# Keys in three chunks of 128 and one of 64 instead of four of 112, with the 64s of two pairs of heads multiplied with their values together on quarters of the array

## The chip, the cores and the metric

One core of one Trainium2 chip runs the kernel. The metric is the device time of one execution in microseconds (us). TensorE (PE) multiplies matrices and has a row of its own for loading weights (PEld); VectorE (DVE), ScalarE (ACT) and GpSimd (POOL) work element by element; SyncE (SP) issues the DMAs of this kernel. Each engine takes its instructions in the order in which the program writes them and waits on semaphores for the others.

## The reference, cut to what matters

```
def _attn_ref(q, k, v):  # 4 batches, 12 heads, 448 positions, 64 wide
    scores = scale * np.matmul(q, k.transpose(0, 1, 3, 2)) - np.log(S)
    attn = 1.0 / (1.0 + np.exp(-scores))
    return np.matmul(attn, v)

x = attn_out, heads side by side: (4, 448, 768)
u = x + token mixing of rank 32 (U, V)        # _moe_ref
x = u + max(u @ w_ch1, 0) @ w_ch2             # 768 -> 3072 -> 768
...                                           # _moe2_ref: theta, cos and sin, two token matrices, w_ch
```

All of it is float32. The change is in the attention and in the small matmuls that the kernel weaves into it. The expression `attn @ v` sums over the 448 keys; in what order the keys stand in the chunks does not matter to that sum, as long as k and v are cut alike.

## The kernel before

The 48 heads are taken as 24 pairs p; a pair's two heads lie on partitions 0 to 63 and 64 to 127. The 448 keys of a pair are four chunks of CP = 112. In the loop over p, TensorE does for each pair:

- `TQ(p + 1)` and `TK(p + 2)`: four transposes each, which turn q and k so that the 64 channels lie on partitions. They write PSUM tiles of the tags `qx` (one bank) and `kk` (two banks), one buffer each; ACT and DVE then split the result into a high and a low part (`kh`, `kl`, `qh`, `ql`).
- `QK(p, half)`: scores of two chunks. Per chunk three products (high by high, high by low, low by high), each as two matmuls, one for each head, on the upper and the lower 64 rows of the array at once. ACT's sigmoid then writes the tile `A` of the chunk. The score tiles (`sc`, two banks) have two buffers.
- `AV(p - 1, c)`: for chunk c two float32 matmuls, one for each head, on the left and the right 64 columns of the array at once. They add up in one PSUM bank (`av`, one buffer) over the four chunks; after the last DVE copies the bank into `X`.
- `XN(p - 2)`: four transposes of `X` into a tile of the tag `qx`, copied by DVE to `xn`.
- In three of the iterations `U1` (24 small matmul rows into the tag `kk`, split by ACT and then by six DVE rows `pc` in `u1_lo`), and in nine (p = 9 to 11, 15 to 17, 21 to 23) `U2`: two matmuls into the two banks of a `kk` tile, which one DVE addition takes into `X`.
- two `early_step()`s: a step each of converting the weights of the next stage (rows L146 to L167 of ACT and DVE, L112 and L115 of POOL).

The order in an iteration is QK half 0, TQ, AV chunks 0 and 1, TK, a step, QK half 1, XN, U1 or U2, AV chunks 2 and 3, `u1_lo`, the loads of pair p + 3, a step. After the loop `split_u(0)` splits batch 0 of X (six rows of ACT, six of DVE), the last pair's four `AV` follow, then `split_u(1)`, `XN(22)`, the first product with w_ch1 (`ch1(0, 0)`), `XN(23)`, and so on. What comes after is the same program in both kernels.

`load_pair(p)` issues on SP, at one place in its order, two DMAs for k, two to four for q and one for v. The pairs 0, 1 and 2, then the U and V matrices, are loaded before the loop; pair 3 is loaded at the end of iteration 0, pair 4 at the end of iteration 1.

The changed lines, as before:

Of the kernel before, what the change touches and what calls it, by code (L numbers as in the profile page):

```python
# [24 lines left out]
def tile_kernel(  # L25
# [15 lines left out]
    nc = tc.nc  # L41
# [66 lines left out]
    def hi_act(o, i):  # L108
        nc.scalar.activation(o, i, AF.Copy)  # L109
# [10 lines left out]
    def lo_dve(o, i, h):  # L120
        nc.vector.tensor_sub(o, i, f(h))  # L121
# [190 lines left out]
    u_in = ap.tile([CP, 2, NC, R], F32, name="u_in")  # L312
    vcat = ap.tile([P, 2, S], F32R, name="vcat")

    q_t, k_t, v_t, qq_t, kk_t, A_t, av_t, xn_t = {}, {}, {}, {}, {}, {}, {}, {}

    def load_pair(p):
        b, hp = divmod(p, NH)
        h0 = 2 * hp
        qt = ap2.tile([CP, NC, 2, D], F32, tag="q", name=f"q_{p}", bufs=3)  # L320
        vt = ap1.tile([CP, 2, NC, D], F32, tag="v", name=f"v_{p}", bufs=4)
        kt = ap2.tile([CP, NC, 2, D], F32, tag="k", name=f"k_{p}", bufs=3)
        for h in range(2):
# [12 lines left out]
        nc.sync.dma_start(
            out=vt.rearrange("p h c d -> p h (c d)"),
            in_=v[b, h0:h0 + 2].rearrange("h (p c) d -> p h (c d)", p=CP),
        )
        q_t[p], k_t[p], v_t[p] = qt, kt, vt  # L340

    def TQ(p):
        ps = ps_a.tile([P, 512], F32, tag="qx", name=f"tq_{p}")
# [10 lines left out]
        qq_t[p] = (h_, l_)  # L354

    def TK(p):
        ps = ps_a.tile([P, 2, 512], F32, tag="kk", name=f"tk_{p}")
        t = k_t.pop(p)
        for c in range(NC):
            nc.tensor.transpose(  # L360
                ps[:, 0, c * CP:(c + 1) * CP], t[:, c].rearrange("p h d -> p (h d)"), ident[:CP, :CP]
            )
        h_ = ap2.tile([P, S], F32R, tag="kh", name=f"kh_{p}", bufs=3)
        l_ = ap2.tile([P, S], F32R, tag="kl", name=f"kl_{p}", bufs=3)
        kk_t[p] = (h_, l_)
        hi_act(h_, ps[:, 0, :S])
        lo_dve(l_, ps[:, 0, :S], h_)

    def QK(p, half):


        (kh, kl), (qh, ql) = kk_t[p], qq_t[p]
        for c in (2 * half, 2 * half + 1):
            ps = ps_b.tile([P, 2, 512], F32, tag="sc", name=f"sc_{p}_{c}", bufs=2)
# [6 lines left out]
            a = ap1.tile([CP, 2, S], F32, tag="A", name=f"A_{p}_{c}", bufs=6)  # L381
            nc.scalar.activation(a, ps[:CP, :, :S], AF.Sigmoid, bias=bias_s[:CP], scale=SCALE)  # L382
            A_t[p, c] = a

    def AV(p, c):
        b, hp = divmod(p, NH)
        if c == 0:
            if p < NP - 1:
                av_t[p] = ps_a.tile([P, 512], F32, tag="av", name=f"av_{p}")
            else:  # L390
                av_t[p] = ps_a.tile([P, 2, 512], F32, tag="kk", name=f"av_{p}")[:, 0]
        ps = av_t[p]
        for h in range(2):
            nc.tensor.matmul(  # L394
                ps[h * D:(h + 1) * D, :S], v_t[p][:, h, c, :], A_t[p, c][:, h, :],
                start=c == 0, stop=c == NC - 1,
            )
        if c == NC - 1:
            nc.vector.tensor_copy(X[:, hp, b * S:(b + 1) * S], ps[:, :S])
# [12 lines left out]
    pc_t, u1_t = {}, []  # L412

    def U1(b, p):
        ps = ps_a.tile([P, 2, 512], F32, tag="kk", name=f"p1_{b}")
        for c in range(NC):
            for g in range(3):
                nc.tensor.matmul(
                    ps[g * R:(g + 1) * R, 1, :2 * P], u_in[:, b % 2, c, :], xn_t[b][:, c, 2 * g * P:2 * (g + 1) * P],
                    start=c == 0, stop=c == NC - 1,  # L420
                )
        o = p.tile([P, DM], F32R, tag="pc", name=f"pc_{b}")
        for g in range(3):
            x = ps[g * R:(g + 1) * R, 1, :2 * P]
            sl = slice(2 * g * P, 2 * (g + 1) * P)
            for m in range(2):
                hi_act(o[m * R:(m + 1) * R, sl], x)
        pc_t[b] = o
        u1_t.append((ps, o))

    def u1_lo():

        while u1_t:
            ps, o = u1_t.pop()
            for g in range(3):
                x = ps[g * R:(g + 1) * R, 1, :2 * P]
# [104 lines left out]
    for p in range(NP):  # L541
        nx = p + 1 < NP
        QK(p, 0)
        if nx:
            TQ(p + 1)
        if p:
            AV(p - 1, 0)
            AV(p - 1, 1)
        if p + 2 < NP:
            TK(p + 2)  # L550
        if p:
            early_step()
# [7 lines left out]
        if b >= 0 and r < NK // 2:  # L560
# [362 lines left out]
```

## Time and profile before

| | us |
|---|---|
| median of 3 runs | 1248.75 (1247.99 to 1248.86) |
| the profiled execution | 1244.25 |
| span of its instructions | 1241.9 |
| attention loop, about | 9 to 202 of the span |
| PE busy | 1213.5 (98%) |

The rows further down come from the profiled execution; times in them are us from the start of its span. In a timeline row stand the start, the length, the engine, the line, the operation, out<-in, the shapes, how many instructions were merged, and in brackets the idle time before it with what ended it. A float32 matmul of `AV` leaves two rows for each instruction, so that one chunk of a pair is four rows. Matmul lengths hold a pipeline's depth, so the distance from start to start is the time that a matmul takes from its engine.

### The profile page before, as it was taken

The numbers are of one execution on the slowest core, as the hardware profiler recorded it, in microseconds if no ns is written. First come the engines' busy times: TensorE is split into PE (matmuls) and PEld (weight loads), VectorE is DVE, ScalarE is ACT, GpSimd is POOL, SyncE is SP. The second block draws the span as 40 slices with busy tenths as digits, with TensorE's granted clock in tenths as the row PEclk, the third lists the DMA queues.
The fourth block names the chain that finished last, engine by engine and source line by source line (L and its number), as shares of the span: only waits on it lengthen the run. The fifth ranks groups of instructions, "written<-read, shape, count | busy, mean of one in ns | idle before, by whom it ended". The sixth has DMA issues, their size and how long they took to land.

```text
span 1241.9 us, 15876 instructions
## 1 busy us (share of the span) xinstructions
PE 1213.5 (98%) x6546; PEld 1051.4 (85%) x6546; DVE 757.5 (61%) x863; ACT 376.4 (30%) x479; POOL 326.7 (26%) x182
## 2 busy tenths in 40 slices
PE   7999999999998989999999999999999999999998
PEld 4555556898888979999999999999999999999998
DVE  3466666458787786777778796967434642731222
ACT  5666665312121221212212121212113531620121
POOL 0112122315243342223324253433200521320000
PEclk9999999999999999999999999999999999999999
DMA  6454541002414141323232323423131000030111
GB/s 162 108 148 105 130 101 51 1 27 77 127 60 144 51 142 41 121 64 98 66 96 77 117 88 116 127 96 89 55 145 51 1 1 1 22 132 1 64 51 64
DMA packets 87783, 99.88 MB, mean 80 GB/s; under 512 B 48416, under 2 KB 77984, under 8 KB 87584
## 3 DMA queue, kind: packets, MB, share of 16 engines
q1 hardware_dynamic: 87712, 98.88, 26.0%
q8 instruction: 51, 0.84, 0.3%
q14 instruction: 20, 0.16, 0.0%
HBM read 80.71 MB, written 18.15 MB: 80 GB/s over the span
## 4 chain that ended last, share of the span: by engine, by line
PE 80%; DVE 10%; issue 8%; DMA 1%; ACT 1%; POOL 1%; SPq 0%; POOLq 0%; ACTq 0%; DVEq 0%
PE g L599 7%; PE g L598 7%; PE g L600 7%; PE y L620 7%; PE y L622 7%; PE y L621 7%; PE av L394 6%; PE sc L378 5%; PE y L810 3%; PE y L811 3%; PE y L809 3%; PE wc L732 2%; PE wc L736 2%; PE wc L733 2%; DVE X L624 2%
## 5 line engine op out<-in xcount | busy, mean ns | idle before, releaser
L620 PE MATMUL y<-gh,w 128*128 128x448 f32 x576 | 213.6, 371 | 16.6 <-DVE X L624 15.1
L622 PE MATMUL y<-gh,w 128*128 128x448 f32 x576 | 212.3, 369 | 0.0
L621 PE MATMUL y<-gl,w 128*128 128x448 f32 x576 | 212.2, 368 | 0.0
L598 PE MATMUL g<-uh,w 128*128 128x448 f32 x576 | 211.3, 367 | 0.0
L599 PE MATMUL g<-ul,w 128*128 128x448 f32 x576 | 211.0, 366 | 0.0
L600 PE MATMUL g<-uh,w 128*128 128x448 f32 x576 | 210.8, 366 | 0.0
L624 DVE TENSOR_TENSOR X<-y,X 128x896 f32<-128x896 f32 x144 | 156.3, 1087 | 87.4 <-PE y L622 86.0
L112 POOL TENSOR_TENSOR ca_w<-ca_w,w 128x768 f32<-128x768 f32 x48 | 94.6, 1970 | 387.4 <-ACT w L109 376.6
L605 ACT ACTIVATE gh<-g 128x896 fp32r<-128x896 f32 x48 | 44.1, 919 | 344.2 <-PE g L600 344.2
L620 PEld LDWEIGHTS y<-gh,w 128*128 128x128 f32 x576 | 109.0, 189 | 28.4 <-DVE X L624 17.9
L622 PEld LDWEIGHTS y<-gh,w 128*128 128x128 f32 x576 | 109.3, 190 | 9.1
L621 PEld LDWEIGHTS y<-gl,w 128*128 128x128 f32 x576 | 109.2, 190 | 8.8
L598 PEld LDWEIGHTS g<-uh,w 128*128 128x128 f32 x576 | 108.6, 189 | 9.4 <-issue 0.4
L599 PEld LDWEIGHTS g<-ul,w 128*128 128x128 f32 x576 | 108.5, 188 | 9.3 <-DVE ul L121 0.4
L600 PEld LDWEIGHTS g<-uh,w 128*128 128x128 f32 x576 | 108.4, 188 | 8.9
L606 DVE SCALAR_TENSOR_TENSOR gl<-g,gh 128x896 fp32r<-128x896 f32 x48 | 52.3, 1089 | 99.2 <-ACT gh L605 99.2
L382 ACT ACTIVATE A<-sc,bias_s 112x896 f32<-112x896 f32 x96 | 91.5, 1003 | 38.6 <-PE sc L378 38.4
L115 POOL TENSOR_TENSOR w<-ca_w,ws_w 128x768 fp32r<-128x768 f32 x48 | 93.4, 1947 | 3.8
L112 POOL TENSOR_TENSOR zl<-t,zh 128x768 fp32r<-128x768 f32 x23 | 42.7, 1878 | 161.3 <-ACT zh L109 161.3
L394 PE MATMUL av<-A,v 112*64 112x448 f32 x384 | 82.3, 551 | 0.0
L121 DVE TENSOR_TENSOR xl<-X,xh 128x768 fp32r<-128x768 f32 x28 | 31.7, 1136 | 67.8 <-ACT xh L109 67.8
L109 ACT ACTIVATE xh<-X 128x768 fp32r<-128x768 f32 x28 | 23.5, 842 | 155.9 <-PE wc L733 92.7
(148 smaller groups left out, 1982.8 us busy)
## 6 DMA issues: line engine op xcount, KB each, us to landing
ws_w<-in_moe_w_ch_dram SPq DMA_DIRECT2D x48, 768.0 KB, 4.6
k<-in_k_dram SPq DMA_DIRECT2D x48, 112.0 KB, 3.4
v<-in_v_dram SPq DMA_DIRECT2D x24, 224.0 KB, 2.9
ws_th<-in_moe_w_theta_dram SPq DMA_DIRECT2D x6, 768.0 KB, 4.4
th_d<-sp_th SPq DMA_DIRECT2D x6, 768.0 KB, 6.9
ws_wc<-in_moe_w_ch_dram SPq DMA_DIRECT2D x6, 768.0 KB, 5.1
wc_d<-sp_wc SPq DMA_DIRECT2D x6, 768.0 KB, 6.9
th_r<-th_d SPq DMA_DIRECT2D x6, 768.0 KB, 4.4
```

Of the source, the lines that this page charges most:

```text
L112: nc.gpsimd.tensor_sub(o, a, b)
L115: nc.gpsimd.tensor_add(o, a, b)
L378: nc.tensor.matmul(ps[:CP, h, :S], a[sl, c * CP:(c + 1) * CP], b[sl], start=n == 0, stop=n == 2)
L382: nc.scalar.activation(a, ps[:CP, :, :S], AF.Sigmoid, bias=bias_s[:CP], scale=SCALE)
L394: nc.tensor.matmul(ps[h * D:(h + 1) * D, :S], v_t[p][:, h, c, :], A_t[p, c][:, h, :], start=c == 0, stop=c == NC - 1,)
L598: nc.tensor.matmul(o, wh[:, sl], uh_t[b][:, kk, :], start=kk == 0, stop=False)
L599: nc.tensor.matmul(o, wh[:, sl], ul_t[b][:, kk, :], start=False, stop=False)
L600: nc.tensor.matmul(o, wl[:, sl], uh_t[b][:, kk, :], start=False, stop=kk == NK - 1)
L620: nc.tensor.matmul(o, wh[:, sl], gh[:, j, :], start=j == 0, stop=False)
L621: nc.tensor.matmul(o, wh[:, sl], gl[:, j, :], start=False, stop=False)
L622: nc.tensor.matmul(o, wl[:, sl], gh[:, j, :], start=False, stop=j == FB - 1)
L624: nc.vector.tensor_add(x, ps[:, :, :S], x)
```

## The change

The keys come as FC = 3 chunks of 128 and one of HC = 64. k and v are loaded in two pieces (a DMA more for k, one more for v in each pair). The 64s of an even pair and of the odd one after it share one tile `Ah` and one tile `vh`, the even pair on partitions 0 to 63, the odd one on 64 to 127. `AV(p, FC)`, called for odd p alone, multiplies both: four matmuls, each with 64 rows and 64 columns, on the four quarters of the array. An even pair's `av` bank therefore stays open until the next pair's iteration; `av` has two buffers now. `kk` shrinks from two banks to one, and `U2` is taken apart: its first matmul writes a `qx` tile and stands between AV chunks 1 and 2, its second a `kk` tile after AV chunk 2, each with a DVE addition of its own. `AV` chunk 1 moves behind QK half 1. After the loop the last pair's chunks come in the order 0, FC, 1, 2; the copy of X for pair 22 now follows FC there.

```diff
     def load_pair(p):
...
-        vt = ap1.tile([CP, 2, NC, D], F32, tag="v", name=f"v_{p}", bufs=4)
-        kt = ap2.tile([CP, NC, 2, D], F32, tag="k", name=f"k_{p}", bufs=3)
+        vt = ap1.tile([P, 2, FC, D], F32, tag="v", name=f"v_{p}", bufs=4)
+        if p % 2 == 0:
+            vh_t[p // 2] = ap1.tile([P, 2, D], F32, tag="vh", name=f"vh_{p}", bufs=3)
+        vh = vh_t[p // 2][p % 2 * HC:(p % 2 + 1) * HC]
+        kt = ap2.tile([P, FC + 1, 2, D], F32, tag="k", name=f"k_{p}", bufs=3)
         for h in range(2):
-            nc.sync.dma_start(out=kt[:, :, h], in_=k[b, h0 + h].rearrange("(p c) d -> p c d", p=CP))
+            nc.sync.dma_start(out=kt[:, :FC, h], in_=k[b, h0 + h, :FC * P].rearrange("(p c) d -> p c d", p=P))
+        nc.sync.dma_start(out=kt[:HC, FC], in_=k[b, h0:h0 + 2, FC * P:].rearrange("h p d -> p h d"))
...
-            in_=v[b, h0:h0 + 2].rearrange("h (p c) d -> p h (c d)", p=CP),
+            in_=v[b, h0:h0 + 2, :FC * P].rearrange("h (p c) d -> p h (c d)", p=P),
         )
+        nc.sync.dma_start(out=vh, in_=v[b, h0:h0 + 2, FC * P:].rearrange("h p d -> p h d"))
...
     def TK(p):
-        for c in range(NC):
+        for c in range(FC + 1):
+            n = keys(c)
             nc.tensor.transpose(
-                ps[:, 0, c * CP:(c + 1) * CP], t[:, c].rearrange("p h d -> p (h d)"), ident[:CP, :CP]
+                ps[:, c * P:c * P + n], t[:n, c].rearrange("p h d -> p (h d)"), ident[:n, :n]
             )
...
     def QK(p, half):
...
-                        ps[:CP, h, :S], a[sl, c * CP:(c + 1) * CP], b[sl], start=n == 0, stop=n == 2
+                        ps[:m, h, :S], a[sl, c * P:c * P + m], b[sl], start=n == 0, stop=n == 2
...
     def AV(p, c):
         for h in range(2):
+            if c < FC:
+                if c == 0 and h == 0:
+                    av_t[p] = ps_a.tile([P, 512], F32, tag="av", name=f"av_{p}", bufs=2)
+                nc.tensor.matmul(
+                    av_t[p][h * D:(h + 1) * D, :S], v_t[p][:, h, c, :], A_t[p, c][:, h, :],
+                    start=c == 0, stop=c == FC - 1 and p % 2 == 1,
+                )
+                continue
+            for e in range(2):
+                sl = slice(e * HC, (e + 1) * HC)
+                nc.tensor.matmul(
+                    av_t[p - 1 + e][h * D:(h + 1) * D, :S], vh_t[p // 2][sl, h, :], Ah_t[p // 2][sl, h, :],
+                    start=False, stop=e == 0,
+                )
+        done = p - 1 if c == FC else p if c == FC - 1 and p % 2 else None
+        if done is not None:
+            b, hp = divmod(done, NH)
+            nc.vector.tensor_copy(X[:, hp, b * S:(b + 1) * S], av_t.pop(done)[:, :S])
...
             AV(p - 1, 0)
-            AV(p - 1, 1)
+            if p % 2 == 0:
+                AV(p - 1, FC)
...
+        if p:
+            AV(p - 1, 1)
...
-            U2(b, 2 * r, ps_a.tile([P, 2, 512], F32, tag="kk", name=f"h_{b}_{r}"), vcat[:, b % 2, :], 2)
+        u2 = b >= 0 and r < NK // 2
+        if u2:
+            U2(b, 2 * r, ps_a.tile([P, 1, 512], F32, tag="qx", name=f"h0_{b}_{r}"), vcat[:, b % 2, :])
         if p:
             AV(p - 1, 2)
-            AV(p - 1, 3)
+        if u2:
+            U2(b, 2 * r + 1, ps_a.tile([P, 1, 512], F32, tag="kk", name=f"h1_{b}_{r}"), vcat[:, b % 2, :])
...
     split_u(0, u01, 0, NK, lo_dve)
-    for c in range(NC):
+    for c in (0, FC, 1, 2):
         AV(NP - 1, c)
```

The order of TensorE from TQ to TK in the iteration of pair 10, before and then now. `av_1091` is pair 9's bank now, `av_1004` pair 8's, which has stood open since the iteration before.

```order
L346 MATMUL tq_1055<-ident,q_937 128x112 x4
L394 MATMUL av_1064<-A_0_958,v_741 64x448 x2
L394 MATMUL av_1064<-A_1_967,v_741 64x448 x2
L360 MATMUL tk_1069<-ident,k_1029 128x112 x4
L378 MATMUL sc_2_1079<-qh_974,kh_872 112x448 x2
```

```order
L357 MATMUL tq_1082<-ident,q_961 128x112 x4
L409 MATMUL av_1091<-A_0_984,v_761 64x448 x2
L416 MATMUL av_1004<-Ah_921,vh_667 64x448
L416 MATMUL av_1091<-Ah_921,vh_667 64x448
L416 MATMUL av_1004<-Ah_921,vh_667 64x448
L416 MATMUL av_1091<-Ah_921,vh_667 64x448
L372 MATMUL tk_1099<-ident,k_1054 128x128 x3
L372 MATMUL tk_1099<-ident,k_1054 128x64
```

Between TQ and TK stood two chunks of one pair; now stand one chunk and the four quarter matmuls, and in the iterations of odd p the one chunk alone.

The order of TensorE from the last score chunk of the same iteration to its end, before and then now (`xt` are XN's transposes, `h` are U2's matmuls).

```order
L378 MATMUL sc_3_1088<-qh_974,kl_873 112x448 x2
L407 MATMUL xt_1097<-ident,X 112x128 x4
L443 MATMUL h_1_1103<-vcat,pc_919 128x448 x2
L394 MATMUL av_1064<-A_2_1001,v_741 64x448 x2
L394 MATMUL av_1064<-A_3_1010,v_741 64x448 x2
L378 MATMUL sc_0_1124<-qh_1060,kh_988 112x448 x2
```

```order
L391 MATMUL sc_2_1109<-qh_1000,kl_897 128x448 x2
L391 MATMUL sc_3_1118<-qh_1000,kh_896 64x448 x2
L391 MATMUL sc_3_1118<-ql_1001,kh_896 64x448 x2
L391 MATMUL sc_3_1118<-qh_1000,kl_897 64x448 x2
L431 MATMUL xt_1127<-ident,X 112x128 x4
L409 MATMUL av_1091<-A_1_993,v_761 64x448 x2
L467 MATMUL h_0_1_1135<-vcat,pc_943 128x448
L409 MATMUL av_1091<-A_2_1025,v_761 64x448 x2
L467 MATMUL h_0_1_1141<-vcat,pc_943 128x448
```

The last chunk of scores has outputs on 64 partitions, after a chunk on 128; and each `h` now stands alone among chunks of `av`.

The order of DVE around the end of the loop, before and then now. `av_2204` is pair 22's bank before and `av_2268` pair 23's; `av_2269` is pair 22's bank now and `av_2331` pair 23's.

```order
L408 COPY xn_1986<-xt_2231 112x4x128
L447 TENSOR_TENSOR X<-h_2_2237,X 128x2x448
L399 COPY X<-av_2204 128x448
L121 TENSOR_TENSOR ul_2255<-X,uh_2254 128x448 x6
L399 COPY X<-av_2268 128x448
L121 TENSOR_TENSOR ul_2284<-X,uh_2283 128x448 x3
```

```order
L432 COPY xn_2046<-xt_2293 112x4x128
L471 TENSOR_TENSOR X<-h_2_2_2301,X 128x448
L471 TENSOR_TENSOR X<-h_2_2_2306,X 128x448
L123 TENSOR_TENSOR ul_2318<-X,uh_2317 128x448 x6
L423 COPY X<-av_2269 128x448
L423 COPY X<-av_2331 128x448
L123 TENSOR_TENSOR ul_2350<-X,uh_2349 128x448 x3
```

The copy of pair 22 into X moved from ahead of the six rows of `split_u(0)` to behind them; `XN(22)` on TensorE reads what it writes.

## Rows read from the trace of the kernel before

**Rows 1.** Stretch 62 to 93 us: us, then busy PE, PEld, DVE, ACT, POOL, clock, DMA.

```profile
62.00:93.00 31.00, 31.00 (x220) 16.06 (x216) 19.78 (x35) 19.03 (x26) 4.56 (x4) 1.00 0.60 148
```

**Rows 2.** Timeline of PE, 102 to 113 us: start, us, engine, line, what.

```profile
102.54 0.65 PE L407 MATMUL xt<-ident,X 128*112 128x128 f32 x4
...
103.52 1.72 PE L394 MATMUL av<-A,v 112*64 112x448 f32 x8
...
107.11 1.72 PE L394 MATMUL av<-A,v 112*64 112x448 f32 x8
108.77 0.60 PE L360 MATMUL tk<-ident,k 112*128 112x112 f32 x4
109.30 0.46 PE L378 MATMUL sc<-qh,kh 64*112 64x448 f32 x2
109.59 0.37 PE L378 MATMUL sc<-ql,kh 64*112 64x448 f32 x2
...
110.41 0.37 PE L378 MATMUL sc<-qh,kl 64*112 64x448 f32 x2
110.71 0.65 PE L407 MATMUL xt<-ident,X 128*112 128x128 f32 x4
111.29 1.72 PE L394 MATMUL av<-A,v 112*64 112x448 f32 x8
```

**Rows 3.** Timeline of PE, 201 to 208 us: the end of the loop.

```profile
201.37 0.65 PE L407 MATMUL xt<-ident,X 128*112 128x128 f32 x4
201.77 0.66 PE L443 MATMUL h<-vcat,pc 128*128 128x448 f32 x2
202.36 4.73 PE L394 MATMUL av<-A,v 112*64 112x448 f32 x24
207.02 0.65 PE L407 MATMUL xt<-ident,X 128*112 128x128 f32 x4
```

**Rows 4.** Timelines of SP's DMA issues, 15 to 36 us.

```profile
15.80 0.42 SPq L289 DMA_DIRECT2D ws_V<-in_moe_V_dram  x1
...
24.02 1.23 SPq L324 DMA_DIRECT2D k<-in_k_dram  x2
...
33.92 1.28 SPq L330 DMA_DIRECT2D q<-in_q_dram  x2
35.24 0.94 SPq L332 DMA_DIRECT2D q<-in_q_dram  x2
```

**Rows 5.** Timeline of PE, 18 to 29 us.

```profile
28.02 0.57 PE L360 MATMUL tk<-ident,k 112*128 112x112 f32 x4 [0.40 <-DMA k<-in_k_dram]
```

**Rows 6.** Timelines of DVE and of PE, 76 to 85 us.

```profile
81.45 2.59 DVE L121 TENSOR_TENSOR pc<-p,pc 32x256 fp32r<-32x256 f32 x6
...
84.24 0.60 PE L360 MATMUL tk<-ident,k 112*128 112x112 f32 x4
```

**Rows 7.** Timelines of PE and of DVE, 133 to 139 us.

```profile
136.78 0.62 PE L407 MATMUL xt<-ident,X 128*112 128x128 f32 x4 [0.82 <-DVE ql L121]
...
137.95 0.68 DVE L408 COPY xn<-xt 112x512 f32<-112x512 f32 x1
```

**Rows 8.** Timeline of DVE, 199 to 222 us.

```profile
202.66 1.08 DVE L447 TENSOR_TENSOR X<-h,X 128x896 f32<-128x896 f32 x1
204.13 0.62 DVE L399 COPY X<-av 128x448 f32<-128x448 f32 x1 [0.39 <-PE av L394]
204.68 6.17 DVE L121 TENSOR_TENSOR ul<-X,uh 128x448 fp32r<-128x448 f32 x6
210.77 0.61 DVE L399 COPY X<-av 128x448 f32<-128x448 f32 x1
```

**Rows 9.** Waits of PE: us in total, times, longest us; then the stretch 302 to 312 us, as Rows 1.

```profile
PE y L620 <- DVE X L624: 15.1, 6, 3.6
...
302.00:312.00 10.00, 7.32 (x30) 6.36 (x29) 9.90 (x9) 1.76 (x2) 7.27 (x4) 0.86 0.38 95
```

**Rows 10.** Timeline of POOL, 285 to 312 us.

```profile
300.35 2.08 POOL L112 TENSOR_TENSOR ca_th<-ca_th,sp_th 128x768 f32<-128x768 f32 x1 [8.21 <-ACT sp_th L109]
```

More of the change, by code (lines that the diff above doesn't have):

```diff
@@ L48, in tile_kernel @@
     NC = S // CP
+    FC = S // P
+    HC = S - FC * P
     NK = DM // P
@@ L313, in tile_kernel @@
     vcat = ap.tile([P, 2, S], F32R, name="vcat")
-    q_t, k_t, v_t, qq_t, kk_t, A_t, av_t, xn_t = {}, {}, {}, {}, {}, {}, {}, {}
+    q_t, k_t, v_t, vh_t, qq_t, kk_t, A_t, Ah_t, av_t, xn_t = ({} for _ in range(10))
     def load_pair(p):
@@ L337, in load_pair, with keys @@
             out=vt.rearrange("p h c d -> p h (c d)"),
-            in_=v[b, h0:h0 + 2].rearrange("h (p c) d -> p h (c d)", p=CP),
+            in_=v[b, h0:h0 + 2, :FC * P].rearrange("h (p c) d -> p h (c d)", p=P),
         )
+        nc.sync.dma_start(out=vh, in_=v[b, h0:h0 + 2, FC * P:].rearrange("h p d -> p h d"))
         q_t[p], k_t[p], v_t[p] = qt, kt, vt
+    def keys(c):
+        return P if c < FC else HC
     def TQ(p):
@@ L356, in TK @@
     def TK(p):
-        ps = ps_a.tile([P, 2, 512], F32, tag="kk", name=f"tk_{p}")
+        ps = ps_a.tile([P, 512], F32, tag="kk", name=f"tk_{p}")
         t = k_t.pop(p)
-        for c in range(NC):
+        for c in range(FC + 1):
+            n = keys(c)
             nc.tensor.transpose(
-                ps[:, 0, c * CP:(c + 1) * CP], t[:, c].rearrange("p h d -> p (h d)"), ident[:CP, :CP]
+                ps[:, c * P:c * P + n], t[:n, c].rearrange("p h d -> p (h d)"), ident[:n, :n]
             )
@@ L365, in TK @@
         kk_t[p] = (h_, l_)
-        hi_act(h_, ps[:, 0, :S])
-        lo_dve(l_, ps[:, 0, :S], h_)
+        hi_act(h_, ps[:, :S])
+        lo_dve(l_, ps[:, :S], h_)
     def QK(p, half):
@@ L373, in QK @@
         for c in (2 * half, 2 * half + 1):
+            m = keys(c)
             ps = ps_b.tile([P, 2, 512], F32, tag="sc", name=f"sc_{p}_{c}", bufs=2)
@@ L378, in QK @@
                     nc.tensor.matmul(
-                        ps[:CP, h, :S], a[sl, c * CP:(c + 1) * CP], b[sl], start=n == 0, stop=n == 2
+                        ps[:m, h, :S], a[sl, c * P:c * P + m], b[sl], start=n == 0, stop=n == 2
                     )
-            a = ap1.tile([CP, 2, S], F32, tag="A", name=f"A_{p}_{c}", bufs=6)
-            nc.scalar.activation(a, ps[:CP, :, :S], AF.Sigmoid, bias=bias_s[:CP], scale=SCALE)
-            A_t[p, c] = a
-    def AV(p, c):
[L386 to L392, printed above, removed]
-        for h in range(2):
[L394 to L399, printed above, removed]
+            if c < FC:
+                a = A_t[p, c] = ap1.tile([P, 2, S], F32, tag="A", name=f"A_{p}_{c}", bufs=5)
+            else:
+                if p % 2 == 0:
+                    Ah_t[p // 2] = ap1.tile([P, 2, S], F32, tag="Ah", name=f"Ah_{p}")
+                a = Ah_t[p // 2][p % 2 * HC:(p % 2 + 1) * HC]
@@ new lines, in QK @@
+            nc.scalar.activation(a, ps[:m, :, :S], AF.Sigmoid, bias=bias_s[:m], scale=SCALE)
+    def AV(p, c):
+        for h in range(2):
+            if c < FC:
+                if c == 0 and h == 0:
[15 more added lines that the diff above has]
+            nc.vector.tensor_copy(X[:, hp, b * S:(b + 1) * S], av_t.pop(done)[:, :S])
@@ L414, in U1 @@
     def U1(b, p):
-        ps = ps_a.tile([P, 2, 512], F32, tag="kk", name=f"p1_{b}")
+        ps = ps_a.tile([P, 512], F32, tag="kk", name=f"p1_{b}")
         for c in range(NC):
@@ L418, in U1 @@
                 nc.tensor.matmul(
-                    ps[g * R:(g + 1) * R, 1, :2 * P], u_in[:, b % 2, c, :], xn_t[b][:, c, 2 * g * P:2 * (g + 1) * P],
+                    ps[g * R:(g + 1) * R, :2 * P], u_in[:, b % 2, c, :], xn_t[b][:, c, 2 * g * P:2 * (g + 1) * P],
                     start=c == 0, stop=c == NC - 1,
@@ L423, in U1 @@
         for g in range(3):
-            x = ps[g * R:(g + 1) * R, 1, :2 * P]
+            x = ps[g * R:(g + 1) * R, :2 * P]
             sl = slice(2 * g * P, 2 * (g + 1) * P)
@@ L435, in u1_lo @@
             for g in range(3):
-                x = ps[g * R:(g + 1) * R, 1, :2 * P]
+                x = ps[g * R:(g + 1) * R, :2 * P]
                 sl = slice(2 * g * P, 2 * (g + 1) * P)
@@ L547, in tile_kernel @@
             AV(p - 1, 0)
-            AV(p - 1, 1)
+            if p % 2 == 0:
+                AV(p - 1, FC)
         if p + 2 < NP:
@@ L558, in tile_kernel @@
             U1(b, ap)
+        if p:
+            AV(p - 1, 1)
         b, r = divmod(p - 3 - NH, NH)
-        if b >= 0 and r < NK // 2:
-            U2(b, 2 * r, ps_a.tile([P, 2, 512], F32, tag="kk", name=f"h_{b}_{r}"), vcat[:, b % 2, :], 2)
+        u2 = b >= 0 and r < NK // 2
+        if u2:
+            U2(b, 2 * r, ps_a.tile([P, 1, 512], F32, tag="qx", name=f"h0_{b}_{r}"), vcat[:, b % 2, :])
         if p:
             AV(p - 1, 2)
-            AV(p - 1, 3)
+        if u2:
+            U2(b, 2 * r + 1, ps_a.tile([P, 1, 512], F32, tag="kk", name=f"h1_{b}_{r}"), vcat[:, b % 2, :])
         u1_lo()
```

## The prediction, made before the changed kernel ran

> **What bounds the kernel now.** I read the stretches first: where the loop over the pairs runs, PE is busy all of the 31 us and no other engine more than 20 [rows 1]. The timeline of PE then shows block after block without a bracket of idle time [rows 2]. So inside the loop the path is PE's own time, and what PE gains or loses there moves the end. There are exceptions, which decide this forecast: PE waits for a transfer at the start of the loop [rows 5], for DVE once in pair 15's iteration [rows 7], and at the end of the loop DVE is the one that is behind [rows 8].
>
> Three prices come from the distances between starts. Of AV, two chunks take 108.77 - 107.11 = 1.66 and six in one block take 207.02 - 202.36 = 4.66 [rows 2, 3]: a chunk costs 0.75, and a block of them 0.16 on top, for filling and emptying the array where the shape of the work changes. Of the scores, two chunks take 110.71 - 109.30 = 1.41 with an inner step of (110.41 - 109.59) / 4 = 0.205: six steps and a fixed 0.18. U2's two matmuls behind XN add 103.52 - 102.54 - 0.58 = 0.40, where 0.58 is XN alone, 110.71 to 111.29 [rows 2].
>
> **The change part by part.**
>
> *AV.* The first block of an iteration falls from two chunks to one, 1.66 to 0.91, which saves 0.75. In iterations of even p the quarters follow. If all four run at once they take one chunk's time, as the two heads' matmuls do now, and a block's fixed part, since their shape is new: 0.91. Only iterations 3 to 23 count, because those before end in a wait for k (next part): 21 x 0.75 = 15.8 saved, 10 x 0.91 = 9.1 spent, **-6.7**.
>
> The page "TensorE: Matmul & The Clock Gate" of the Trainium skill, section "Measured speedup vs the span model", puts several tiles at one matmul's length and some 4 ns a tile; no row here shows four quarters, and by it the 0.91 stands.
>
> *The start.* Each pair's load has two DMAs more. SP issues without a pause until k of pair 4, at 24.02, and TK(4) starts at 28.02, when that k lands, after a wait of 0.40 [rows 4, 5]. Eight of the new issues (pairs 0 to 3) stand ahead of it. They move 64 rows of two heads, as q's first pieces in the odd batches do, which step by (35.24 - 33.92) / 2 = 0.66 [rows 4]: 8 x 0.66 = **+5.3**. From below, the shortest issue there is 0.42: 3.4. From above 5.6, if the last transpose of TK(4) waits for its own small piece. A gain is excluded, nothing leaves the queue. PE itself would be there earlier: TK(3) slips by six issues, 4.0, and what lies between takes what it took, so the slack grows by about 1.3. Later the queue waits for buffers, and the two issues a pair hide behind PE.
>
> *The last chunk of scores.* Its outputs stand on 64 partitions, the chunk ahead on 128. The trace has no such change within QK. Every change of shape it has costs the fixed part, and the nearest is one of width alone: from TQ (128 columns) into AV (64). I take the full 0.18 for 22 iterations, **+4.0**; the other end is nothing, if 64 rows to 64 rows is no change at all. A gain is excluded: the step of 0.205 belongs to 448 columns of input, which stay.
>
> "TensorEngine Tiling (Array Packing)" of the Trainium skill, section "Key Properties", says that changing the tiling mode drains the array while changing the tile does not. By it 64x128 to 64x64 is a change of mode and the term is 4.0; read as a change of tile, it is 0. No row settles it, and it speaks against this change.
>
> *U2 taken apart.* Now XN 0.58, two AV blocks of one chunk 0.91 each, and each h alone, a step and an emptying, 0.205 + 0.09 = 0.29: 2.98. Before 0.98 + 1.66 = 2.64. In eight iterations (the ninth is in the last part), 8 x 0.34 = **+2.7**; up to 2.9, if each h pays the full fixed part once more in a few.
>
> *TK.* Four transposes of the same 448 columns in all, the last in another shape. The scores behind share that shape, so one change is moved rather than added: **+0.4**, between 0 and 20 x 0.09 = 1.8.
>
> *Waits for DVE in the loop.* After U1 the six `pc` rows hold the `kk` bank until 81.45 + 2.59 = 84.04, and TK starts at 84.24 [rows 6]. With the shorter block TK comes 0.75 earlier and the `pc` rows do not, since they follow U1: about 0.7 of the saving goes back in iterations 9, 15 and 21, 2.1. In iteration 15 XN waits for `ql` until 136.78 [rows 7], and `ql` again doesn't move; but there TK's loss only replaces that wait, so I add nothing. The first h now needs the `qx` bank, which XN's copy must empty. In iteration 15 that copy ends at 137.95 + 0.68 = 138.63, and h would come at 136.78 + 0.58 + 0.91 = 138.27: 0.4. Iterations 17 and 9 have the same two conversion rows ahead of the copy: 0.5 and 0.2. Where XN runs free again, a tenth is lost here and there. Together **+3.3**, between 2 and 4.
>
> *The end of the loop.* XN(22) needs X of pair 22. That copy now stands behind six rows of `split_u(0)`, 6.17 us [rows 8]. Counted from XN(21) at 201.37: XN, AV, h, AV, h end 2.98 later, at 204.35. The second addition starts some 0.2 after its matmul's end, as now (201.77 + 0.66 = 202.43 against 202.66), and with 0.62 ends near 205.3. Six rows to 211.4, the copy to 212.0, XN(22) at 212.1. Before it started at 207.02 [rows 3]: 5.1 later. The first product waited some 0.2 for `ul` before, which is no longer so: **+4.9** (4.2 to 5.2). PE's own AV work there ends near 207.8 and hides in it. Nothing behind gives it back but the rival below.
>
> *The clock.* That leaves PE idle for 4.3 us. The longest of PE's later waits is 3.6 us, and the 10 us around one of them show a granted clock of 0.86 [rows 9]: 2.8 us at the lower of its two levels, 1.2 against 2.4 GHz, or 1.4 us of work lost at most. **+1.0**, between 0 and 1.8.
>
> **The sum:** -6.7 + 5.3 + 4.0 + 2.7 + 0.4 + 3.3 + 4.9 + 1.0 = +14.9. On the profiled execution's 1244.25 that is 1259.2. The median of the runs shown is 4.5 higher; on it, 1248.75 + 14.9 = 1263.7. All low ends give +5.6, 1254.4, and all high ends +18.7, 1267.4.
>
> **The rivals.**
>
> *The quarters run two at a time.* The trace shows two halves at once, by rows (scores) and by columns (AV), never both. If two quarters of a column can't run together, each block takes 0.75 more in ten iterations (at both ends of the loop it is hidden), 7.5: 1271. For it: two banks are written on the same partitions at once. Against it: the scores do just that now, at the full step of 0.205. This is also the case in which the change doesn't do what it says, since AV would then be worth nothing: 15.8 saved, 16.6 spent.
>
> *The lateness is given back.* Behind the loop PE waits six times for DVE's additions, 15.1 us [rows 9]. If what ends these waits runs ahead on its own, apart from PE, a later PE waits less there, and all of +14.9 could vanish: 1248.6, no change; with the low ends of the sum 1239, faster. It decides from the point at which the conversions on POOL and DVE are already behind when the loop ends. Against it: POOL has stood idle for 8.21 us before its row at 300.35 [rows 10], so it isn't working off a backlog; its work comes with the products' own progress.
>
> **How the numbers follow.** The forecast as summed, 1254 to 1268: 0.78. Quarters two at a time, 1262 to 1274: 0.10. Given back, 1239 to 1251: 0.10. Anything else 0.02. The likeliest gives 1263.7. A range of 1254 to 1269 leaves out the case of giving back and the larger part of the quarters' case, 0.18 in all. A measurement of this kernel tells 0.2%, 2.5 us, from no change. Faster 0.05 and same 0.06 come from the case of giving back and a corner of the rest, slower 0.89.
>
> **What would show it.** In the trace after: TK(4) near 33 instead of 28; two chunks of scores apart by one changed step, 1.59 in place of 1.41; a block of quarters of 0.9, not 1.7; a lone h of 0.3; XN(22) near 221 instead of 207.02 (the terms of the loop make 9.0, its own part 5.1), after a wait of about 4 us for a copy on DVE. The six waits still at about 15 us. I am wrong if TK(4) comes before 31, if XN(22) doesn't wait, or if those six waits shrink.

## The result

The changed kernel takes 1256.5 us, the median of five runs (1254.8 to 1258.9), where the kernel before has 1248.75. The ratio of the paired runs is 1.008, with a 95% interval of 1.0058 to 1.0102. Run again beside the experiments below, it took 1256.7 against 1243.8, a ratio of 1.0107 (1.0085 to 1.0129). So the change costs about 1%, 8 to 13 us between medians, and the forecast's side and range hold: the range was 1254 to 1269, and 1263.7 was called the likeliest.

The profiled execution took 1257.49 us, with a span of 1255.7, against 1244.25 and 1241.9 before. Four starts on PE divide those 13.8 us, and the prediction's sum can be divided at the same places:

| stretch on PE | before, us | after, us | difference | predicted |
|---|---|---|---|---|
| up to TK(4) | 28.02 | 33.49 | +5.5 | +5.3 |
| TK(4) to XN(21) | 173.35 | 175.11 | +1.8 | +3.7 |
| XN(21) to XN(22) | 5.65 | 10.53 | +4.9 | +5.1 |
| XN(22) to XN(23) | 8.11 | 9.36 | +1.3 | +0.8 |
| XN(23) to the end of the span | 1026.8 | 1027.2 | +0.4 | 0 |
| sum | 1241.9 | 1255.7 | +13.8 | +14.9 |

A second profile of each kernel, from the repeated runs below, gives +5.6, +1.8, +4.9 and +1.3 in the first four rows.

The waits of PE in the changed kernel (engine, line, what it waited for: us in total, times, longest us):

```profile
PE y L649 <- DVE X L653: 15.4, 6, 3.6
PE tk L372 <- DMA k<-in_k_dram: 5.6, 2, 3.9
PE xt L431 <- DVE X L423: 3.8, 1, 3.8
PE tk L372 <- DVE pc L123: 1.6, 3, 0.5
...
PE h L467 <- DVE xn L432: 1.4, 3, 0.6
...
PE xt L431 <- DVE ql L123: 1.0, 1, 1.0
```

The first row answers to [rows 9]: 15.1 us has become 15.4, so nothing of the delay is given back behind the loop; the second profiles have 13.9 and 14.4. The others are at the places that the prediction named, except that the longest wait for k stands one pair earlier, before TK(3).

**The start.** TK(3) in the kernel before:

```profile
20.41 0.57 PE L360 MATMUL tk<-ident,k 112*128 112x112 f32 x4 [1.48 <-DMA k<-in_k_dram]
```

The issues of k for pairs 3 and 4 on SP, and then PE's timeline, in the changed kernel:

```profile
20.45 1.23 SPq L329 DMA_DIRECT2D k<-in_k_dram  x2
...
29.68 1.23 SPq L329 DMA_DIRECT2D k<-in_k_dram  x2
```

```profile
23.78 1.17 PE L372 MATMUL tk<-ident,k 128*128 128x128 f32 x4 [3.86 <-DMA k<-in_k_dram]
...
27.22 2.56 PE L409 MATMUL av<-A,v 128*64 128x448 f32 x8
...
31.67 0.97 PE L409 MATMUL av<-A,v 128*64 128x448 f32 x4
32.58 0.98 PE L416 MATMUL av<-Ah,vh 64*64 64x448 f32 x8
33.49 0.75 PE L372 MATMUL tk<-ident,k 128*128 128x128 f32 x4
```

K of pair 4 is issued 29.68 - 24.02 = 5.7 us later than before [rows 4], and TK(4) starts 5.5 us later [rows 5]. But TK(4) doesn't wait for that k. The wait stands one pair earlier: PE waits 3.86 us for k before TK(3), and the row of two chunks of AV behind it is 2.56 us long, where [rows 2] have 1.72. The last three rows also show the new block: the quarters (`Ah`, eight matmuls) take 33.49 - 32.58 = 0.91 us, as one chunk alone does (32.58 - 31.67 = 0.91). Four quarters run at once.

The granted clock of these stretches in the changed kernel (start and end, us, busy PE, PEld, DVE, ACT, POOL, clock, DMA share, GB/s):

```profile
22.00:30.00 8.00, 6.22 (x26) 3.44 (x28) 1.12 (x3) 2.89 (x4) 0.00 (x0) 0.57 0.52 130
...
220.00:224.00 4.00, 4.00 (x13) 3.56 (x13) 1.81 (x4) 0.00 (x0) 0.00 (x0) 0.57 0.00 0
```

A clock of 0.57 means that TensorE ran for most of the stretch at the lower of its two levels, 1.2 GHz. It did so behind the 3.86 us of idle time before TK(3), and behind the 3.81 us before XN(22).

**The end of the loop**, PE and then DVE of the changed kernel:

```profile
208.60 0.65 PE L431 MATMUL xt<-ident,X 128*112 128x128 f32 x4
...
210.08 0.47 PE L467 MATMUL h<-vcat,pc 128*128 128x448 f32 x1
210.48 0.97 PE L409 MATMUL av<-A,v 128*64 128x448 f32 x4
...
211.78 0.97 PE L409 MATMUL av<-A,v 128*64 128x448 f32 x4
...
219.13 0.65 PE L431 MATMUL xt<-ident,X 128*112 128x128 f32 x4 [3.81 <-DVE X L423]
...
228.49 0.60 PE L431 MATMUL xt<-ident,X 128*112 128x128 f32 x4
```

```profile
212.43 6.11 DVE L123 TENSOR_TENSOR ul<-X,uh 128x448 fp32r<-128x448 f32 x6
218.46 1.14 DVE L423 COPY X<-av 128x448 f32<-128x448 f32 x2
```

As forecast, the copy of X that XN(22) needs stands behind the six `ul` rows, in place of ahead of them as in [rows 8]; PE takes its work in order and waits 3.81 us. A lone h (one of U2's matmuls that stands by itself) is 210.48 - 210.08 = 0.40, not 0.29.

### The profile page after: what moved, and what is told of

Same layout as the page of the kernel before. It is cut to its first block, busy times and chain, and to the rows that moved or that the text cites. A ratio compares the mean times of both kernels' runs of the same rounds, so it can differ in the third digit from the quotient of the medians.

```text
span 1255.7 us, 15874 instructions
## 1 busy us (share of the span) xinstructions
PE 1217.8 (97%) x6546; PEld 1054.1 (84%) x6546; DVE 758.1 (60%) x872; ACT 377.9 (30%) x479; POOL 324.6 (26%) x182
## 4 chain that ended last, share of the span: by engine, by line
PE 78%; DVE 11%; issue 8%; SPq 1%; ACT 1%; POOL 1%; DMA 0%; DVEq 0%; POOLq 0%; ACTq 0%
PE g L628 7%; PE g L627 7%; PE g L629 7%; PE y L649 7%; PE y L651 7%; PE y L650 7%; PE sc L391 4%; PE av L409 4%; PE y L839 3%; PE y L840 3%; PE y L838 3%; PE wc L761 2%; PE wc L765 2%; PE wc L762 2%; DVE X L653 2%
## 5 line engine op out<-in xcount | busy, mean ns | idle before, releaser
L649 PE MATMUL y<-gh,w 128*128 128x448 f32 x576 | 213.3, 370 | 16.7 <-DVE X L653 15.4
L400 ACT ACTIVATE A<-sc,bias_s 128x896 f32<-128x896 f32 x72 | 70.0, 1005 | 41.9 <-PE sc L391 41.5
L409 PE MATMUL av<-A,v 128*64 128x448 f32 x288 | 67.5, 566 | 0.0
```

Of the source, the lines that this page charges most:

```text
L400: nc.scalar.activation(a, ps[:m, :, :S], AF.Sigmoid, bias=bias_s[:m], scale=SCALE)
L409: nc.tensor.matmul(av_t[p][h * D:(h + 1) * D, :S], v_t[p][:, h, c, :], A_t[p, c][:, h, :], start=c == 0, stop=c == FC - 1 and p % 2 == 1,)
L649: nc.tensor.matmul(o, wh[:, sl], gh[:, j, :], start=j == 0, stop=False)
```

## The experiments

**Before and after again.** Two kernels were run unchanged, to see how far one profile can be trusted.

> The kernel before, unchanged, against itself: where do the 4.5 us lie that separate its shown run of 1244.4 from the others (1248 to 1249), of which the changed kernel's profile shows no trace? If they lie in one place (theory: a stretch of a few us at the low granted clock that some executions have and others lack, as the starts of the changed kernel do), a second profile of about 1248 shows one such stretch more than the three after the start in the first, 1.5 to 3.4 us long each. Rival: they lie at the ends, outside the span, and the span is again 1241.9. The ratio should be 1.000 with an interval of about 0.002.

It took 1243.57 us, a ratio of 0.9992 (0.9977 to 1.0007) to the other runs of before, whose median here is 1244.95. Its span is 1245.9, 4.0 longer than in the first profile, yet XN(23) starts at 215.25, as before (215.13). Both expectations fall: the mean granted clock is no lower (0.996, before 0.994), and the 4 us are not at the ends. They lie spread over the products of the two layers behind the attention. PE's row of two stretches, in the first profile of before and then in this one (us, PE busy and its matmuls, clock, DMA share, GB/s):

```profile
750.00:800.00 50.00, 50.00 (x248) 1.00 0.28 95
850.00:900.00 50.00, 50.00 (x249) 1.00 0.21 65
```

```profile
750.00:800.00 50.00, 50.00 (x244) 1.00 0.28 95
850.00:900.00 50.00, 50.00 (x244) 1.00 0.15 48
```

In the same 50 us, busy throughout at a granted clock of 1.00, PE makes 244 matmuls instead of 248 or 249. The median distance between two starts is 207 ns in these stretches of the second profile and 203 in the first, and both profiles of either kernel have stretches of both kinds.

> The changed kernel, unchanged, beside the kernel before and the three variants of the same call. Between profiles it is 13.2 us slower than before, between medians 7.8. Theory (the 13 us are real, and the medians differ less because single executions of either kernel run long stretches of the two-layer part at a step of 207 instead of 203 ns): ratio 1.008 to 1.011, 1255 to 1258.5 where before has 1245. Rival (the profile of before was a lucky one by 4 us and the true difference is about 8): ratio 1.0055 to 1.007.

1256.74 us beside 1243.82, ratio 1.0107 (1.0085 to 1.0129), span 1256.2. The theory holds: the cost is about 13 us, and the first set of runs of before, four of five at 1248 to 1249, was longer than the later ones.

**The last score chunk, widened.**

```diff
-            m = keys(c)
+            m, k0 = keys(c), min(c * P, S - P)
...
-                        ps[:m, h, :S], a[sl, c * P:c * P + m], b[sl], start=n == 0, stop=n == 2
+                        ps[:, h, :S], a[sl, k0:k0 + P], b[sl], start=n == 0, stop=n == 2
```

> The changed kernel with the last score product of each pair made on 128 outputs (keys 320 to 447) instead of 64 (keys 384 to 447), so that the array's shape does not change between the two products of the first half; the last 64 rows of weights then come from the wrong keys. Theory (going from 64x128 to 64x64 costs nothing: the step across it was 0.206 like its neighbours): QK's first half stays at about 2.9 us for its two products and the time within 1 us of the changed kernel, at most the 0.065 per pair, 1.6 us, by which the second half's first product is longer. Rival, the prediction's own term (each change of shape costs up to 0.17): 4.0 us less.

1255.37 us, 1.0093 (1.0073 to 1.0112): 1.4 us less than the changed kernel beside it, with intervals that overlap. From TK(4) to XN(21) it takes 208.87 - 33.61 = 175.26 us, the changed kernel 175.11. TK and the scores of QK half 1 behind it (the half that holds the last chunk; the expectation calls it the first), in the changed kernel and then in this one:

```profile
121.35 0.75 PE L372 MATMUL tk<-ident,k 128*128 128x128 f32 x4
121.83 0.53 PE L391 MATMUL sc<-qh,kh 64*128 64x448 f32 x2
...
122.34 0.43 PE L391 MATMUL sc<-qh,kl 64*128 64x448 f32 x2
122.55 0.42 PE L391 MATMUL sc<-qh,kh 64*64 64x448 f32 x2
...
123.30 0.65 PE L431 MATMUL xt<-ident,X 128*112 128x128 f32 x4
```

```profile
122.00 0.53 PE L391 MATMUL sc<-qh,kh 64*128 64x448 f32 x2
...
122.52 0.43 PE L391 MATMUL sc<-qh,kl 64*128 64x448 f32 x2
122.72 0.43 PE L391 MATMUL sc<-qh,kh 64*128 64x448 f32 x2
```

The step from 64*128 to 64*64 is 122.55 - 122.34 = 0.21, and the step at the same place without a change of shape is 122.72 - 122.52 = 0.20. The change of shape costs nothing that these rows can show; the prediction's 4.0 us were not there.

**The two h products together again.**

```diff
-        if u2:
-            U2(b, 2 * r, ...)
         if p:
             AV(p - 1, 2)
+        if u2:
+            U2(b, 2 * r, ...)
         if u2:
             U2(b, 2 * r + 1, ...)
```

> The changed kernel with the two h products of an iteration of U2 kept together behind the third product, as they stood in the kernel before, instead of one h alone behind each. Theory (a lone h costs 0.40 where two in a row cost 0.45 together, and three of them wait 1.4 us for the copy of xn): 0.35 in each of nine iterations and most of the 1.4, 3.0 to 4.5 us less, near 1252.5 to 1253.5. Rival (the waits move to the next user of the same bank, the transposes of q, since the last copy comes later): 1.5 to 2.5 us less. Second rival (a lone h is no dearer than one of a pair): under 0.5 us less.

1253.79 us, 1.0061 (1.0033 to 1.0088), against 1.0107 for the changed kernel. From TK(4) to XN(21) it takes 204.94 - 34.22 = 170.72 us instead of 175.11: 4.4 less, as the theory has it, and the wait of h for xn is gone from the list of waits. At the end of the loop the low clock took part of that back: XN(22) to XN(23) is 10.5 us here, 9.4 in the changed kernel. So this edit is worth 4.4 us in its own stretch, and about 3 between medians (1253.79 against 1256.5 and 1256.7).

**XN(22) between the halves of a chunk.**

```diff
+    ch1(0, 0, (0,))
     XN(NP - 2)
-    ch1(0, 0)
+    ch1(0, 0, (1,))
```

> The changed kernel with XN(22) moved from behind both halves of the last chunk but one to between its halves, so that PE has a half chunk of products while DVE does the six ul rows and the copy of X. Theory (end of loop: +4.9 of wait and work before XN(22), and 1.3 more in the low clock that follows the 3.8 us of idle): 5 to 6 us less than the changed kernel, 1250.5 to 1251.5 when that runs at 1256.5. Rival (whatever is late there is given back by the waits of y for X behind it, so that removing it only lets those waits grow from 15.4 to about 20): 0 to 1 us less.

1252.33 us, 1.006 (1.0039 to 1.0082). XN(22) starts without a wait, and XN(21) to XN(23) takes 14.7 us (209.30 to 224.03) instead of 19.9: 5.2 less. The six waits of y stay, at 14.3 us. No other wait takes the place of the one that is gone. So of the 4.9 + 1.3 = 6.2 us that the end of the loop lost, 5.2 were this wait and the low clock behind it, and they were on the path; the medians show 4.2 to 4.4.

**Why the copy of X is late.**

```diff
-    split_u(1, u01, 0, NK, lo_pool, lo_dve)
+    split_u(1, u01, 0, NK, lo_dve)
```

> The changed kernel with that last edit alone: the six rows ul of the second batch all on DVE, none on POOL. Theory (XN(22) waits 3.8 us because three of the six rows ahead of the copies of X on DVE take 1.56 instead of 0.61 us beside POOL's rows): six rows in 3.3 instead of 6.1 us, XN(22) 2.8 us earlier, and 2.8 to 4.1 us less in all (the second if the low clock behind the wait goes too), 1252.5 to 1254. Rival (ACT's uh is the limit, one row each 0.47 us and other work ahead of it): XN(22) less than 1 us earlier and the time unchanged.

1251.96 us, 1.0066 (1.0047 to 1.0085). DVE of this kernel:

```profile
212.06 3.29 DVE L123 TENSOR_TENSOR ul<-X,uh 128x448 fp32r<-128x448 f32 x6
215.27 1.15 DVE L423 COPY X<-av 128x448 f32<-128x448 f32 x2
216.34 3.29 DVE L123 TENSOR_TENSOR ul<-X,uh 128x448 fp32r<-128x448 f32 x6
```

Six rows take 3.29 us instead of 6.11 (6.17 in [rows 8]), XN(22) waits 1.0 instead of 3.8, and XN(21) to XN(23) takes 223.73 - 208.22 = 15.5 us instead of 19.9. The theory's 2.8 to 4.1 were 4.4. So nearly half of DVE's time there was not work: in the changed kernel POOL ran three `ul` rows of the second batch beside three of DVE's. One row of DVE, over all rows of the line (shortest, median, longest ns), in the changed kernel and then in this one:

```profile
L123 DVE TENSOR_TENSOR ul<-X,uh x9: 615/618/1566, 212.4 to 220.6; 128x448 fp32r<-128x448 f32 x9
```

```profile
L123 DVE TENSOR_TENSOR ul<-X,uh x12: 610/614/619, 212.1 to 219.0; 128x448 fp32r<-128x448 f32 x12
```

The Trainium skill's page "SBUF — State Buffer", section "SBUF: two separate sides", says that DVE, when it reads two inputs from SBUF, and GpSimd take a shared pair of ports in turns, each for a whole instruction. The rows agree: 0.62 us alone, 1.57 beside a POOL row of that kind.

**The start: the small loads on another queue.**

```diff
+        small = nc.scalar if p < 4 else nc.sync
-        nc.sync.dma_start(out=kt[:HC, FC], ...)
+        small.dma_start(out=kt[:HC, FC], ...)
...
-        nc.sync.dma_start(out=vh, ...)
+        small.dma_start(out=vh, ...)
```

> The changed kernel with the small loads of k and v of the first four pairs issued on ACT's queue instead of SP's, so that SP issues as many transfers before k of pair 4 as in the kernel before. Theory (eight extra issues on SP make k of pairs 3 and 4 late, and the idle time before TK(3) brings low clock behind it): TK(3) waits about 1.5 instead of 3.9 us, TK(4) starts near 28 instead of 33.5, and the time is 5 to 5.5 less, near 1251. Rival 1 (it is the transfers themselves, more and smaller, not their issue, that make k late): TK(3) still waits 3 us or more and the time is less than 2 us shorter. Rival 2 (the issues now delay ACT's first splits by 8 times 0.6): 0 to 3 us shorter with ACT as the new releaser at the start.

1252.21 us, 1.0055 (1.0035 to 1.0076). TK(4) starts at 30.10, 3.4 us earlier and not 5.5. SP and then PE of this kernel:

```profile
17.45 1.21 SPq L329 DMA_DIRECT2D k<-in_k_dram  x2
```

```profile
21.14 0.72 PE L373 MATMUL tk<-ident,k 128*128 128x128 f32 x4 [3.32 <-DMA k<-in_k_dram]
...
23.60 2.79 PE L410 MATMUL av<-A,v 128*64 128x448 f32 x8
```

TK(3) comes within 0.7 us of its place in the kernel before (20.41), but still waits 3.32 us, since PE now reaches it 1.1 us sooner (17.82 against 18.93): in the kernel before the same wait was 1.48. Of the 2.1 us by which TK(4) is still later than before, 0.7 are TK(3)'s. The way from TK(3) to TK(4) makes the rest, 8.96 us where it was 7.61, with the low clock behind the wait (a row of 2.79 us for two chunks of AV).

The first sign of rival 1 came true, its price did not. From the issue of pair 3's k to TK(3) it takes 20.41 - 16.34 = 4.07 us in the kernel before, 23.78 - 20.45 = 3.33 in the changed one and 21.14 - 17.45 = 3.69 here: the transfers have not become slower, k lands late because it is issued late. Here too it is issued 1.1 us later than before, although as many issues stand ahead of it on SP.

**The three together.**

> All three edits at once: small loads of the first four pairs on ACT's queue, the two h products together, XN(22) between the halves. In the single profiles XN(23) started 4.5, 3.3 and 2.5 us earlier by them. Theory (three separate losses, so the savings add): 10 to 11 us less than the changed kernel, about 1245 to 1247 where before has 1245, and the six waits of y for X still 14 to 15 us. Rival (the savings were clock and chance, or the next wait takes their place): 5 us less or fewer, 1251 or more.

1242.73 us, 0.9988 (0.9972 to 1.0005). That is 14 us less than the changed kernel beside it, and more than the 10 to 11 expected; XN(22) and h wait no more, the six waits stay at 14.9 us. XN(23) of this kernel:

```profile
217.16 0.60 PE L432 MATMUL xt<-ident,X 128*112 128x128 f32 x4
```

It starts 228.49 - 217.16 = 11.3 us earlier than in the changed kernel, where the three single profiles make 10.3, so the savings add. Between medians the three places held the whole loss. In this profile XN(23) is still 2.0 us later than before (215.13), since the start is not cured: TK(4) stands at 31.77. This makes the change level with the kernel before, not better.

**SP's order.** The same with another order on SP's queue:

```diff
     load_pair(2)
-    seq[0].load()
-    seq[1].load()
...
         if p + 2 < NP:
             TK(p + 2)
-        if p:
+        if p > 2:
             early_step()
...
             load_pair(p + 3)
-        if p:
+        if p == 1:
+            seq[0].load()
+            seq[1].load()
+        for _ in range(0 if p < 3 else 2 if p in (4, 5, 6) else 1):
             early_step()
```

> All three edits of the kernel above, and the 13 loads of U and the first V moved on SP's queue from ahead of the loads of pair 3 to behind those of pair 4 (the preparing of U, V and the first weights then begins at pair 3 instead of pair 1, with two steps more in pairs 4, 5 and 6). It tells whether the idle time before TK(3) and the low clock behind it come from SP's order alone. Theory: no wait of TK(3) for k above 1 us, TK(4) near 26 to 27 us where before has 28.0 and the changed kernel 33.5, and 3 us less than the kernel with the three edits, 1242 to 1244 where before has 1245. Rival (the transfers themselves are the limit at the start): TK(3) still waits 2 us or more, and the time is that of the kernel with the three edits.

1243.53 us, 0.9992 (0.9979 to 1.0006). PE of this kernel:

```profile
17.80 0.75 PE L373 MATMUL tk<-ident,k 128*128 128x128 f32 x4
19.76 1.72 PE L410 MATMUL av<-A,v 128*64 128x448 f32 x8
...
25.19 0.75 PE L373 MATMUL tk<-ident,k 128*128 128x128 f32 x4
...
206.60 0.47 PE L630 MATMUL g<-ul,w 128*128 128x448 f32 x1 [0.62 <-DVE ul L123]
```

The start behaves as the theory says: TK(3) doesn't wait, two chunks of AV take 1.72, and TK(4) starts at 25.19, 2.8 us ahead of the kernel before. So the wait of TK(3) came from what stands ahead of its k in SP's order. The gain did not reach the end, though: XN(21) starts at 197.98, 4.5 us earlier than with the three edits (202.46), XN(23) at 214.79 only 2.4 earlier, and the medians show none of it (ratios of 0.9992 and 0.9988). With the loop ending earlier against POOL's work, DVE's six `ul` rows ran beside POOL rows for longer and took 8.26 us, and PE waited for them three times, 1.9 us in all:

```profile
201.80 8.26 DVE L123 TENSOR_TENSOR ul<-X,uh 128x448 fp32r<-128x448 f32 x6
```

**All five edits.** To that, the row that puts the second batch's `ul` on DVE, as above.

> The kernel with the three edits and the other order on SP's queue, and now all six rows ul of the second batch on DVE, so that POOL has none while DVE makes the six of the first. In the kernel without this last edit those six took 8.26 us in its profile and PE waited three times for them, 1.9 us in all; one row took 0.61 us alone and 1.56 while a POOL row ran beside it. Theory (DVE and POOL get in each other's way): six rows in 3.5 to 4.6 us, no wait of g for ul, and 2 us less, 1240.5 to 1242 where before has 1244: a ratio of 0.997 to 0.998. Rival (the rows are slow for another reason, such as ACT's writes of uh into the same tile): six rows in 6 us or more and the time unchanged at a ratio of 0.999.

1241.02 us, 0.9979 (0.9965 to 0.9993). The six rows take 5.39 us, more than expected, for POOL still converts a weight beside the first of them; no product waits for `ul`. The ratio is as expected, but its interval overlaps that of the kernel without this edit (0.9979 to 1.0006).

**What of that is the chunks'.** The last two edits, made to the kernel before:

> The kernel before with the two edits that have nothing to do with the chunks: the other order of the loads of U and V on SP's queue, and the six rows ul of the second batch on DVE. It tells whether the kernel with all five edits (0.998 of before) is faster through the chunks or through these two. Theory 1 (chunks of 128 with quarters are a gain once their side effects are gone: 0.26 us an iteration, less 3 us of waits for DVE that remain): this kernel stays at 0.999 to 1.001 of before, and the one with five edits is 2 us or more ahead of it. Theory 2 (what the chunks save is taken by those waits, and the gain is the order's): TK(4) near 26 instead of 28, and this kernel too is at 0.997 to 0.9985, no slower than the one with five edits.

> The kernel with all five edits again, beside the one above on the same chip and with the same runs of before: 0.998 as measured before (0.9965 to 0.9993). Theory 1: 2 us or more faster than the kernel with the two edits alone; theory 2: the same within 1 us, or slower.

The kernel before with two edits takes 1241.40 us, 0.9974 (0.9956 to 0.9991); the changed kernel with five takes 1240.57, 0.9966 (0.9948 to 0.9984). Theory 2 holds. TK(4) and XN(23) of the first, and then XN(23) of the second:

```profile
25.61 0.60 PE L360 MATMUL tk<-ident,k 112*128 112x112 f32 x4
...
212.79 0.60 PE L407 MATMUL xt<-ident,X 128*112 128x128 f32 x4
```

```profile
212.87 0.60 PE L432 MATMUL xt<-ident,X 128*112 128x128 f32 x4
```

The two XN(23) stand 0.1 us apart. Both kernels beat the two of this case. In the kernel before with two edits TK(4) starts 28.02 - 25.61 = 2.4 us earlier than before, and XN(23) 215.13 - 212.79 = 2.3 earlier. So what is gained lies at the start, where only the order was changed, and of the chunks no gain can be measured. With them the stretch from TK(4) to XN(21) is 0.8 us shorter (172.92 against 173.73), with 4.4 us of waits of PE in it against 1.0, and that from XN(21) to XN(23) is 0.7 longer (14.19 against 13.45).

## Why the prediction was right, and where not

The side, the range and the places of the loss were right. In the sum, two terms were mis-sized and one step of the start was wrong.

**AV** was right in its price. The quarters run four at once, 0.91 us, and the rival in which they run two at a time falls. No run measures the term of -6.7 alone; the loop below shows it together with the scores and TK.

**The last chunk of scores** is the term that failed: +4.0 predicted, nothing found. With it fails the prediction's rule that a block pays 0.16 to 0.18 wherever the shape changes. The rule had been read from changes that include the rows of the array or a change between transposing and multiplying. Within 64 rows, going from 128 columns to 64 is free. The Trainium skill's page "TensorEngine Tiling (Array Packing)", section "Key Properties", which says that a change of tiling mode drains the array, was read as a warning here. The 0.21 against 0.20 shows no price of that for this change. TK's +0.4 was nothing either: its own block goes from 0.53 [rows 2] to 121.83 - 121.35 = 0.48, and the scores behind it take 123.30 - 121.83 = 1.47 instead of 1.41.

The loop shows both. Three starts of XN in the kernel before (its second profile) and in the changed kernel, two iterations without U2:

```profile
110.90 0.65 PE L407 MATMUL xt<-ident,X 128*112 128x128 f32 x4
118.68 0.65 PE L407 MATMUL xt<-ident,X 128*112 128x128 f32 x4
126.44 0.65 PE L407 MATMUL xt<-ident,X 128*112 128x128 f32 x4
```

```profile
116.25 0.65 PE L431 MATMUL xt<-ident,X 128*112 128x128 f32 x4
...
123.30 0.65 PE L431 MATMUL xt<-ident,X 128*112 128x128 f32 x4
...
131.27 0.65 PE L431 MATMUL xt<-ident,X 128*112 128x128 f32 x4
```

15.54 us become 15.02: 0.26 less for each pair, about 5.5 over 21 iterations, where AV, scores and TK together were put at -6.7 + 4.0 + 0.4 = -2.3.

**U2 taken apart** was too small: 0.34 an iteration and 2.7 in all, with 0.29 for a lone h. It is 0.40, and two of them add 0.80 where the pair added 0.40 [rows 2]; the two chunks of AV, now in two blocks, add 0.15. From 208.60 to 211.78 it is 3.18 us, where it was 2.64: 0.54, and 4.3 in eight iterations. In the experiment with the h products together the same stretch takes 207.78 - 204.94 = 2.84, 0.34 less; eight of these and the 1.4 of waits of h are the 4.1 of the 4.4 us that it gave back.

**The waits for DVE** were right: +3.3 predicted, and 1.6 + 1.4 + (1.0 - 0.8) = 3.2 in the list of waits. With these the loop comes to -5.5 + 4.3 + 3.2 = +2.0, against 1.8 in the table.

**The start** was right in size, 5.5 for 5.3. Wrong was that what lies between TK(3) and TK(4) takes what it took, so that PE's slack in front of TK(4) grows by 1.3. TK(3) came 3.4 us later (the prediction had 4.0), and the way from it to TK(4) took 9.71 us instead of 7.61, with the low clock behind the wait. The issues alone would have given nearly the same. In the experiment with the `ul` rows, whose start is the same, k of pair 4 is issued at 29.76, and TK(4) does wait for it:

```profile
33.17 0.72 PE L372 MATMUL tk<-ident,k 128*128 128x128 f32 x4 [0.57 <-DMA k<-in_k_dram]
```

That is 5.2 later than before, as the prediction has it. In the changed kernel the low clock put it at 33.49, and in three other profiles with the same start at 33.87 to 34.22. That the low clock added so little to the 5.3 is luck: with the 7.39 us that the way takes without it (25.19 - 17.80 in the kernel with the other order), PE would have been at TK(4) near 31.2, an estimate, and would have waited there for that k.

**The end of the loop and the clock** were right: XN(22) starts after 3.81 us of waiting for a DVE copy, 4.9 later by its own part, and 1.3 behind it. What the prediction took as fixed, 6.17 us for six rows, was nearly half waiting for POOL. **The lateness given back** falls: the six waits went from 15.1 to 15.4, and in the second profiles from 13.9 to 14.4.

**The number.** The sum gave 1259.2 on the profiled run's time, and 1257.5 and 1256.7 were measured. The step to the median added 4.5 us that the later runs of before don't show: their medians are 1243.5 to 1245. (Longer stretches at a step of 207 ns would do that; those runs have no trace that could tell.) So 1263.7 is too high by this and by the two terms, -3.2 for the loop's shapes and +1.6 for U2, of which the second hid half of the first. That the sum of +14.9 came so near to the +13.8 of the profiles is in part this luck. (The high ends of the terms add up to +18.6, not +18.7.)

## What to carry to other kernels

Price a change of shape by which part of the array's shape changes, and look for that very change in the trace before charging it. Count a change's small DMAs on the queue that issues them, and a matmul that loses its neighbour as dearer. When a change's gain is on the engine that bounds the kernel, ask who feeds it: here 5.5 us of shorter PE work were outweighed by U2's lone matmuls, by a queue's order and by waits for DVE, and another order was worth more than the change.

## What the runs showed of the hardware that I had not expected

- The step between matmuls of the same form is 203 ns in some stretches of an execution and 207 in others, both at a granted clock of 1.00 (248 and 244 matmuls in 50 us). Over 200 us this makes 4 us. What sets it, no run here tells.
- A DVE row with two inputs in SBUF takes 0.62 us alone and 1.57 beside a POOL row of the same form, and up to 2.28 beside POOL's conversion of a weight. With POOL's three rows given to DVE too, DVE was done with all twelve and the copies of X 7.6 us after the first began; in the changed kernel, with nine, it took 8.8.
- From weights of 64*128 to weights of 64*64 the step between score matmuls is the usual 0.20 to 0.21 us.
- Idle time of PE cost more than itself: the 3.86 us of it before TK(3) were followed by about 5 us of work at the lower clock (a granted clock of 0.57 from 22 to 30 us), which made the 7.61 us from TK(3) to TK(4) into 9.71.
